# FFN of six batches as two-by-two blocks with seven products instead of eight, in float32, in a funnel attention and routed FFN kernel

## The chip, the cores and the metric

The kernel runs on one core of a Trainium2 chip. The metric is the device time of a launch in microseconds. TensorE multiplies matrices, VectorE, ScalarE and GpSimd work on elements, SyncE issues most DMAs. The profile's names for them are PE (with PEld for its weight loads), DVE, ACT, POOL and SP.

## The reference

Attention over pooled queries for 8 batches of 8 heads, then a feed-forward network (FFN) for the 128 tokens of each batch that a gate scores highest.

```python
# q, k, v: (8, 8, 1152, 64); w_gate (512), w1 (512, 1024), w2 (1024, 512); capacity 128; all float32
q_pool = q.reshape(B, H, S // 2, 2, D).mean(axis=3)
attn = softmax(scale * q_pool @ k.T)                 # 576 queries, 1152 keys
x = (attn @ v)  as (B, 576, 512)
scores = x @ w_gate
for b in range(B):
    top_idx = the 128 tokens with the highest scores[b]
    h = np.maximum(x[b, top_idx] @ w1, 0.0)          # 128 x 512 by 512 x 1024
    ye = h @ w2                                      # 128 x 1024 by 1024 x 512
    g = 1.0 / (1.0 + np.exp(-scores[b, top_idx]))
    out[b, top_idx] = x[b, top_idx] + g[:, None] * ye
```

## The kernel before

The main loop runs over 64 halves: two for each of the 32 pairs of heads (8 batches of 4 pairs). In half h, TensorE computes the scores of half h and then the weighted sums of half h-1. ScalarE takes exponentials from PSUM into `p` and copies the weighted sums out (`two`). GpSimd adds up exponentials (`acc`) for the softmax sums and adds the two parts of the weighted sums (`av`). VectorE folds the sums and transposes. Each batch's routing and FFN is a generator; `units()` advances every such generator by one step per half, up to its next true mark. Batch 5's second layer is held back for the end, where the last two batches' routing would otherwise leave TensorE idle. The function `pieces` then interleaves the three remaining generators: `older` (batch 5), `old` (batch 6) and `new` (batch 7). Each engine executes its instructions in the order in which this code emits them. Parts that the change and the prediction touch:

```python
        self.const = pool("const", 1)
        self.load = pool("load", 2)
        self.work = pool("work", 2)
        self.small = pool("small", 4)
        self.ffn = pool("ffn", 2)
        self.dram = pool("dram", 2, space=bass.MemoryType.DRAM)
        psum = bass.MemoryType.PSUM
        self.psum = pool("psum", 4, space=psum)
    # ... cut ...
    def load_pair(self, b, hp):

        nc = self.nc
        kb = self.load.tile([P, self.KB, BLK], F32, name="kb")
        qb = self.load.tile([P, self.QB, 2, BLK], F32, name="qb")
    # ... cut ...
        nc = self.nc
        qp = self.load.tile([P, self.QB, BLK], F32, name="qp", bufs=1)
        kT = pair["kT"] = self.load.tile([P, self.S], F32, name="kT")
        qT = pair["qT"] = self.load.tile([P, self.Sp], F32, name="qT")
        nc.gpsimd.tensor_tensor(
            out=qp[:, :, :], in0=pair["q"][:, :, 0, :], in1=pair["q"][:, :, 1, :], op=ALU.add
        )
        nc.vector.transpose(
            kT.rearrange("p (c g i) -> p c g i", c=self.NC, i=BLK),
            pair["k"].rearrange("p (g c) d -> p c g d", c=self.NC),
        )
        nc.vector.transpose(qT[:, :], qp.rearrange("p n d -> p (n d)"))
    # ... cut ...
        for c in range(self.NC):
            sc = self.banks()
            for e in range(2):
                keys = slice(e * self.D, (e + 1) * self.D)
                for j in range(2):
                    rows = slice(j * self.D, (j + 1) * self.D)
                    nc.tensor.matmul(
                        sc[keys, j, 0:n],
                        lhsT=pair["kT"][rows, c * P + keys.start : c * P + keys.stop],
                        rhs=pair["qT"][rows, qs],
                        start=True,
                        stop=True,
                    )
            nc.scalar.activation(p[:, c // G, c % G, :, :], sc[:, :, 0:n], AF.Exp, scale=self.scale)
    # ... cut ...
        two = self.small.tile([P, 2, n], F32, name="two", bufs=2)
        nc.scalar.copy(two[:, :, :], av[:, :, 0:n])
        half["av"] = self.small.tile([P, n], F32, name="av", bufs=2)
        nc.gpsimd.tensor_tensor(
            out=half["av"][:, :], in0=two[:, 0, :], in1=two[:, 1, :], op=ALU.add
        )
    # ... cut ...
            hT = ffn.tile([P, self.NFC, P], F32, name="hT")
            for f0 in range(0, self.NFC, 4):
                pv = self.banks()[:, 0, :].rearrange("p (c n) -> p c n", n=P)
                for f in range(4):
                    for c in range(self.ND):
                        nc.tensor.matmul(
                            pv[:, f, 0:w],
                            lhsT=self.w1[:, c, (f0 + f) * P : (f0 + f + 1) * P],
                            rhs=xeT[:, c, 0:w],
                            start=(c == 0),
                            stop=(c == self.ND - 1),
                        )
                    if f == 3:
                        nc.scalar.activation(hT[:, f0 : f0 + 4, 0:w], pv[:, :, 0:w], AF.Relu)
                    yield "hidden" if f0 + f == self.NFC - 1 else False
    # ... cut ...
            ps = self.banks()[:, 0, :]
            for f in range(self.NFC):
                nc.tensor.matmul(
                    ps[0:w, 0 : self.Dm],
                    lhsT=hT[:, f, 0:w],
                    rhs=self.w2[:, f, :],
                    start=(f == 0),
                    stop=(f == self.NFC - 1),
                )
                yield False
    # ... cut ...
                y = ffn.tile([P, self.Dm], F32, name="y", bufs=1)
                nc.scalar.activation(
                    y[0:w, :], ps[0:w, 0 : self.Dm], AF.Copy, scale=own_gate[0:w, 0:1]
                )
                nc.gpsimd.tensor_tensor(out=xe[0:w, :], in0=y[0:w, :], in1=xe[0:w, :], op=ALU.add)
            nc.gpsimd.indirect_dma_start(
    # ... cut ...
    def units(self):

        for entry in self.routing[::-1]:
            b, unit = entry
            if b in self.waiting:
                continue
            end = next((mark for mark in unit if mark), None)
            if end is None:
                self.routing.remove(entry)
            elif end == "hidden" and b == self.B - 3:
                self.waiting.add(b)
    # ... cut ...
                    if pair["hp"] == 0:
                        part = self.ffn.tile([P, self.NPAIR, self.QB], F32, name="part")
                    pair["part"] = part
                else:
                    loaded = None
                    if n + 2 < len(pairs):
                        loaded = self.load_pair(*pairs[n + 2])
                        self.load_values(loaded)
                    if n > 1:
                        self.stored(halves[h - 4]["pair"])
                if h > 1:
                    next(weights, None)
                half = {"pair": pair, "s": s}
                halves.append(half)
                self.scores(half)
                if h > 1:

                    of = halves[h - 2 - s]["pair"]
                    if s == 0:
                        of["groups"] = self.side_by_side(of["sum"].rearrange("p j n -> p (j n)"))
                    else:
                        self.spread(of)
                if h > 2:
                    self.gated(halves[h - 3])
                self.folded(half)
                if h > 1:
                    self.multiplied(halves[h - 2])
                if s == 0 and loaded:
                    upcoming = loaded
                    self.prepare_pair(upcoming)
            else:
                self.stored(halves[h - 3]["pair"])
                self.gated(halves[h - 3])
                self.multiplied(halves[h - 2])
                self.units()
            if h > 0:
                done = halves[h - 1]
                self.weighted(done)
                self.drained(done)
            if h == n_halves:
                self.multiplied(done)
                self.gated(halves[h - 2])
            if 1 < h < n_halves and s == 0:
                done["pair"]["total"] = self.added(done["pair"]["groups"])
            if h == n_halves:
                self.normalized(done["pair"])
            elif h > 2 and s == 1:
                self.normalized(halves[h - 2]["pair"])
            if h < n_halves:
                self.units()
    # ... cut ...
        pieces(older, self.NFC - 2)
        pieces(new, 1)
        pieces(older, 2)
        pieces(new, 3)
        pieces(older)
        pieces(old, self.NFC)
        pieces(new, 1)
        low = self.counted()
        pieces(old, self.NFC - 3)
        pieces(new, 2)
        pieces(old)
        count = self.outside(low)
        pieces(new)
```

## Time and profile before

| what | value |
|---|---|
| time, median of 3 runs (range) | 711.05 us (709.72 to 711.47) |
| span of the profiled execution, granted TensorE clock | 706.3 us, 0.999 |
| TensorE busy from 20 to 60, 200 to 600 us | all of it |
| TensorE busy from 690 to the end | 9.72 of 16.30 us |
| DMA | 82.86 MB, 376,640 of 389,490 packets under 512 B |
| exponentials (L825) | 576 of 128x576, 319.2 us |
| FFN layer 1 (L1203), layer 2 (L1216) on TensorE | 59.3 and 57.3 us |

A group line of the profile has the line of the kernel, the engine, the operation, output and inputs by name, shapes, the number of records, then busy microseconds, the mean nanoseconds of one, and the idle time of the engine before them with what ended it. A timeline line has the start, the time it takes, and the same names; "x72" means that 72 records in a row were merged. TensorE's ends are modelled, so its durations overlap.

### The profile page before, as it was taken

What the parts mean: (1) busy time and instruction counts of PE and PEld (TensorE: products, weight loads), DVE (VectorE), ACT (ScalarE), POOL (GpSimd) and SP (SyncE); (2) the same over time, 40 slices, a digit from 0 to 9 for tenths busy, and PEclk for the clock granted to TensorE, in tenths of its full rate; (3) what the DMA queues carried; (4) which work ended last, traced back from release to release, by engine and by line L of the source; (5) the groups of instructions that cost most, each with busy time, mean ns of one, the idle gap of its engine ahead of it and who ended that gap; (6) DMA issues with size and microseconds to landing.
All of it is one profiled execution on the core that took longest, in us unless ns stands there. A gap on an engine that the chain in (4) does not pass through costs nothing.

```text
span 706.3 us, 23391 instructions
## 1 busy us (share of the span) xinstructions
PE 695.8 (99%) x9948; PEld 499.9 (71%) x9948; DVE 494.4 (70%) x793; ACT 442.8 (63%) x963; POOL 484.9 (69%) x452
## 2 busy tenths in 40 slices
PE   8999999999999999999999999999999999999996
PEld 5668889977857678577775777767776677767573
DVE  3877777896549965499654987549784597869540
ACT  6677777777547774477745777467754777577210
POOL 5877777877668685586955879557884777866520
PEclk9999999999999999999999999999999999999999
DMA  9888887849692296825867258652877428442200
GB/s 181 172 170 181 182 166 139 151 95 164 116 169 57 66 165 126 154 52 106 166 104 135 52 126 159 119 106 52 163 127 134 86 53 172 72 82 60 47 31 35
DMA packets 389490, 82.86 MB, mean 117 GB/s; under 512 B 376640, under 2 KB 376640, under 8 KB 389376
## 3 DMA queue, kind: packets, MB, share of 16 engines
q1 hardware_dynamic: 387872, 76.49, 57.4%
q0 software_dynamic: 1280, 4.20, 1.7%
q8 instruction: 80, 1.31, 0.8%
q10 hardware_dynamic: 224, 0.59, 0.3%
q14 instruction: 34, 0.28, 0.1%
HBM read 69.65 MB, written 11.59 MB: 115 GB/s over the span
## 4 chain that ended last, share of the span: by engine, by line
PE 92%; POOL 3%; issue 1%; DVE 1%; DMA 1%; ACT 1%; SPq 0%; POOLq 0%; DVEq 0%; ACTq 0%
PE ps L818 38%; PE ps L836 37%; PE ps L1203 8%; PE ps L1216 7%; POOL acc L857 2%; DMA kb<-in_k_dram 1%; PE ps L1192 1%; POOL prod L925 0%; ACT p L825 0%; POOL x L956 0%; DVE fold L862 0%; POOL av L846 0%; SPq L759 0%; PE ps L1147 0%; PE ps L1053 0%
## 5 line engine op out<-in xcount | busy, mean ns | idle before, releaser
L825 ACT ACTIVATE p<-ps 128x576 f32<-128x576 f32 x576 | 319.2, 691 | 2.6 <-PE ps L818 2.3
L857 POOL TENSOR_TENSOR acc<-p 128x576 f32<-128x576 f32 x192 | 266.1, 1413 | 50.4 <-ACT p L825 50.0
L818 PE MATMUL ps<-qT,kT 64*64 64x288 f32 x4608 | 296.0, 405 | 0.3 <-ACT p L825 0.3
L836 PE MATMUL ps<-p,v_sb 64*64 64x288 f32 x4608 | 294.1, 403 | 0.0
L836 PEld LDWEIGHTS ps<-p,v_sb 64*64 64x64 f32 x4608 | 213.2, 133 | 67.8 <-ACT p L825 14.3
L818 PEld LDWEIGHTS ps<-qT,kT 64*64 64x64 f32 x4608 | 193.3, 132 | 89.8 <-ACT p L825 18.5
L862 DVE TRANSPOSE_TENSOR_REDUCE fold<-p 128x54 f32<-128x1728 f32 x64 | 126.0, 1969 | 117.2 <-ACT p L825 117.2
L862 DVE TRANSPOSE_TENSOR_REDUCE fold<-acc 128x54 f32<-128x1728 f32 x64 | 124.8, 1951 | 42.0 <-POOL acc L857 41.9
L844 ACT COPY two<-ps 128x576 f32<-128x576 f32 x64 | 40.9, 638 | 126.1 <-PE ps L836 113.2
L846 POOL TENSOR_TENSOR av<-two 128x288 f32<-128x288 f32 x64 | 51.1, 798 | 28.9 <-ACT two L844 27.3
L956 POOL TENSOR_TENSOR x<-avb,rec 128x576 f32<-128x576 f32 x32 | 37.0, 1157 | 43.1 <-DVE rec L954 27.1
L1203 PEld LDWEIGHTS ps<-xeT,w 128*128 128x128 f32 x512 | 57.8, 192 | 2.7 <-issue 2.6
L1203 PE MATMUL ps<-xeT,w 128*128 128x128 f32 x512 | 59.3, 277 | 0.0
L1216 PE MATMUL ps<-w,hT 128*128 128x512 f32 x128 | 57.3, 598 | 0.0
L925 POOL TENSOR_TENSOR prod<-avb,w_gate 128x288 f32<-128x288 f32 x64 | 51.3, 802 | 0.6 <-DVE avb L915 0.6
L902 ACT ACTIVATE sums<-total,tiny 32x18 f32<-32x18 f32 x124 | 38.2, 308 | 13.1 <-DVE total L893 11.4
L732 POOL TENSOR_TENSOR qp<-qb 128x576 f32<-128x576 f32 x31 | 43.8, 1412 | 2.5 <-DMA qb<-in_q_dram 2.5
L1216 PEld LDWEIGHTS ps<-w,hT 128*128 128x128 f32 x128 | 23.6, 190 | 28.1 <-issue 28.0
L735 DVE STREAM_TRANSPOSE kT<-kb 128x1152 f32<-128x1152 f32 x31 | 42.5, 1369 | 0.0
L1211 ACT ACTIVATE hT<-ps 128x512 f32<-128x512 f32 x16 | 9.6, 597 | 47.7 <-PE ps L1203 47.7
L1238 POOL TENSOR_TENSOR xe<-y,xe 128x512 f32<-128x512 f32 x7 | 8.9, 1270 | 38.3 <-ACT y L1235 38.3
L915 DVE STREAM_TRANSPOSE avb<-av 128x288 f32<-128x288 f32 x64 | 29.2, 456 | 7.2 <-POOL av L846 7.2
(95 smaller groups left out, 326.1 us busy)
## 6 DMA issues: line engine op xcount, KB each, us to landing
kb<-in_k_dram SPq DMA_DIRECT2D x124, 144.0 KB, 3.6
qb<-in_q_dram SPq DMA_DIRECT2D x124, 144.0 KB, 3.9
v_sb<-in_v_dram SPq DMA_DIRECT2D x124, 144.0 KB, 3.4
out_dram<-x SPq DMA_DIRECT2D x128, 72.0 KB, 3.0
lines<-row_rank SPq DMA_DIRECT2D x7, 640.0 KB, 4.1
w<-in_moe_w_dram SPq DMA_DIRECT2D x8, 512.0 KB, 4.8
sc_row<-row SPq DMA_DIRECT2D x7, 288.0 KB, 3.4
acc<-in_q_dram ACTq DMA_DIRECT2D x2, 288.0 KB, 4.2
```

The lines of the kernel that those rows point to most:

```text
L732: nc.gpsimd.tensor_tensor(out=qp[:, :, :], in0=pair["q"][:, :, 0, :], in1=pair["q"][:, :, 1, :], op=ALU.add)
L735: nc.vector.transpose(kT.rearrange("p (c g i) -> p c g i", c=self.NC, i=BLK), pair["k"].rearrange("p (g c) d -> p c g d", c=self.NC),)
L818: nc.tensor.matmul(sc[keys, j, 0:n], lhsT=pair["kT"][rows, c * P + keys.start : c * P + keys.stop], rhs=pair["qT"][rows, qs], start=True, ...
L825: nc.scalar.activation(p[:, c // G, c % G, :, :], sc[:, :, 0:n], AF.Exp, scale=self.scale)
L836: nc.tensor.matmul(av[j * self.D : (j + 1) * self.D, e, 0:n], lhsT=half["pair"]["v"][keys, j, c, :], rhs=half["p"][keys, c // G, c % G, j, :],
L844: nc.scalar.copy(two[:, :, :], av[:, :, 0:n])
L846: nc.gpsimd.tensor_tensor(out=half["av"][:, :], in0=two[:, 0, :], in1=two[:, 1, :], op=ALU.add)
L857: nc.gpsimd.tensor_tensor(out=acc[:, u, :], in0=units[:, 0, u, :], in1=units[:, 1, u, :], op=ALU.add)
L862: nc.vector.tensor_reduce(fold[:, a, :], of.rearrange("p u (m d) -> p (u m) d", d=BLK), AX.X, ALU.add, apply_transpose=True,)
L925: self.nc.gpsimd.tensor_tensor(out=pair["prod"][:, ns, :], in0=pair["avb"][:, ns, :], in1=self.w_gate[:, hp : hp + 1, :].broadcast_to([P, ...
L1203: nc.tensor.matmul(pv[:, f, 0:w], lhsT=self.w1[:, c, (f0 + f) * P : (f0 + f + 1) * P], rhs=xeT[:, c, 0:w], start=(c == 0), stop=(c == self ...
L1216: nc.tensor.matmul(ps[0:w, 0 : self.Dm], lhsT=hT[:, f, 0:w], rhs=self.w2[:, f, :], start=(f == 0), stop=(f == self.NFC - 1),)
```

## The change

Six of the eight batches' FFN is done for two batches at a time. The tokens of two batches are stacked into a matrix of 256 rows, and each of the two layers is a product of two matrices that are cut into two-by-two blocks. Such a product has eight block products; it can be written with seven, for sums and differences of blocks (Winograd's form of Strassen's scheme), all in float32. The sums of the weights (`tw`) are computed once by VectorE, kept in DRAM, and loaded for each layer; the sums of the inputs (`s`) are computed by GpSimd for each layer; ScalarE copies each product out of PSUM, and VectorE adds them in SBUF. Relu and the gate's scaling are separate ScalarE instructions on SBUF. To make room in SBUF, several tiles lose a buffer: `kb` and `qb` go from two to one, `v_sb` from three to two, `two`, `prod` and `sc_row` from two to one; V is loaded for the next pair instead of the one after it. Batches 4 and 5 now hold back their second layer together for the end, and the order of the pieces there is new. Batches 6 and 7 are computed as before. The purpose is to take multiplications off TensorE.

```diff
+
+        self.paired = self.B - 2 - self.B % 2
+        self.tw = self.const.tile([P, 4, self.ND // 2 * self.F // 2], F32, name="tw")
+        self.tw_kept = {}
 ... cut ...
 
+    def quarter(self, layer, i, j):
+
+        w, rows, columns = (self.w1, self.ND, self.F) if layer == 1 else (self.w2, self.NFC, self.Dm)
+        of = slice(i * rows // 2, (i + 1) * rows // 2), slice(j * columns // 2, (j + 1) * columns // 2)
+        return w[:, of[0], of[1]]
+
+    def summed(self, layer, i):
+        c = (self.ND if layer == 1 else self.NFC) // 2
+        return self.tw[:, i, :].rearrange("p (c n) -> p c n", c=c)
+
+    def weight_sums(self):
+
+        nc = self.nc
+        for layer in (2, 1):
+            b11, b12, b21, b22 = (self.quarter(layer, i, j) for i in range(2) for j in range(2))
+            t1, t2, t3, t4 = (self.summed(layer, i) for i in range(4))
+            kept = self.tw_kept[layer] = self.dram.tile(
+                [P, 4, self.tw.shape[-1]], F32, name=f"tw{layer}", bufs=1
+            )
+            for i, (to, x, y) in enumerate(((t1, b12, b11), (t2, b22, t1), (t3, b22, b12), (t4, b21, t2))):
+                nc.vector.tensor_tensor(out=to, in0=x, in1=y, op=ALU.subtract)
+                nc.sync.dma_start(kept[:, i, :], self.tw[:, i, :])
+                yield
+
+    def load_sums(self, layer):
+        for i in range(0, 4, 2):
+            self.nc.sync.dma_start(self.tw[:, i : i + 2, :], self.tw_kept[layer][:, i : i + 2, :])
+            yield
+
 
 
     def load_pair(self, b, hp):
 
         nc = self.nc
-        kb = self.load.tile([P, self.KB, BLK], F32, name="kb")
-        qb = self.load.tile([P, self.QB, 2, BLK], F32, name="qb")
+        kb = self.load.tile([P, self.KB, BLK], F32, name="kb", bufs=1)
+        qb = self.load.tile([P, self.QB, 2, BLK], F32, name="qb", bufs=1)
 ... cut ...
-        v_sb = pair["v"] = self.load.tile([P, 2, self.NC, self.D], F32, name="v_sb", bufs=3)
+        v_sb = pair["v"] = self.load.tile([P, 2, self.NC, self.D], F32, name="v_sb", bufs=2)
 ... cut ...
-        two = self.small.tile([P, 2, n], F32, name="two", bufs=2)
+        two = self.small.tile([P, 2, n], F32, name="two", bufs=1)
 ... cut ...
+            token = {"xe": xe, "xeT": xeT, "gate": own_gate, "index": index, "rows": rows_out, "w": w, "b": b}
+            if b >= self.paired:
+                yield from self.layers(token)
+            elif b % 2 == 0:
+                self.first_of_two = token
             else:
-                y = ffn.tile([P, self.Dm], F32, name="y", bufs=1)
-                nc.scalar.activation(
-                    y[0:w, :], ps[0:w, 0 : self.Dm], AF.Copy, scale=own_gate[0:w, 0:1]
-                )
-                nc.gpsimd.tensor_tensor(out=xe[0:w, :], in0=y[0:w, :], in1=xe[0:w, :], op=ALU.add)
-            nc.gpsimd.indirect_dma_start(
-                out=rows_out,
-                out_offset=bass.IndirectOffsetOnAxis(ap=index[0:w, 0:1], axis=0),
-                in_=xe[0:w, :],
-                in_offset=None,
-                bounds_check=(b + 1) * Sp - 1,
-                oob_is_err=False,
-            )
+                yield from self.layers_of_two([self.first_of_two, token])
 ... cut ...
+    def room_of_sums(self, c, w):
+        s = self.ffn.tile([P, 4, self.NFC // 2, P], F32, name="s", bufs=1)
+        return s, [s[:, i, 0:c, 0:w] for i in range(4)]
+
+    def input_sums(self, a, s):
+
+        a11, a12, a21, a22 = a
+        s1, s2, s3, s4 = s
+        add, subtract = ALU.add, ALU.subtract
+        for i, (to, x, y, op) in enumerate(
+            ((s1, a21, a22, add), (s2, s1, a11, subtract), (s3, a11, a21, subtract), (s4, a12, s2, subtract))
+        ):
+            self.nc.gpsimd.tensor_tensor(out=to, in0=x, in1=y, op=op)
+            if i % 2:
+                yield i == 3
+
+    def seven_products(self, layer, a, s, c, rest, shape):
+
+
+
+        nc = self.nc
+        (a11, a12, _, a22), (s1, s2, s3, s4), (c11, c12, c21, c22) = a, s, c
+        b11, b21, b22 = (self.quarter(layer, i, j) for i, j in ((0, 0), (1, 0), (1, 1)))
+        t1, t2, t3, t4 = (self.summed(layer, i) for i in range(4))
+        u, x, y = rest
+
+        steps = (
+            (a11, b11, c11, ()),
+            (s2, t2, u, ((u, c11),)),
+            (s3, t3, c21, ((c21, u),)),
+            (s1, t1, c22, ((u, c22), (c22, c21))),
+            (s4, b22, c12, ((c12, u),)),
+            (a12, b21, x, ((c11, x),)),
+            (a22, t4, y, ((c21, y),)),
+        )
+        for i, (of, by, to, sums) in enumerate(steps):
+            if i % 2 == 0:
+                tile = self.banks()
+            ps, n = shape(tile[:, i % 2, :]), of.shape[1]
+            for f in range(by.shape[2] // P if layer == 1 else 1):
+                for k in range(n):
+                    if layer == 1:
+                        args = ps[:, f, :], by[:, k, f * P : (f + 1) * P], of[:, k, :]
+                    else:
+                        args = ps, of[:, k, :], by[:, k, :]
+                    nc.tensor.matmul(
+                        args[0], lhsT=args[1], rhs=args[2], start=k == 0, stop=k == n - 1
+                    )
+            nc.scalar.copy(to, ps)
+            for to, of in sums:
+                nc.vector.tensor_tensor(out=to, in0=to, in1=of, op=ALU.add)
+            yield i == len(steps) - 1
+
+    def layers_of_two(self, tokens):
 ... cut ...
+        a = quarters([token["xeT"] for token in tokens], self.ND // 2)
+        _, s = self.room_of_sums(self.ND // 2, w)
+        for _ in self.input_sums(a, s):
             yield True
+        hidden = [ffn.tile([P, self.NFC, P], F32, name="hT") for _ in tokens]
+        c = quarters(hidden, self.NFC // 2)
+        rest = [ffn.tile([P, 512], F32, name="u", bufs=1)]
+        rest += [ffn.tile([P, 512], F32, name="y") for _ in range(2)]
+        yield from self.seven_products(1, a, s, c, [lines(tile) for tile in rest], lines)
+        for tile in hidden:
+            nc.scalar.activation(tile[:, :, 0:w], tile[:, :, 0:w], AF.Relu)
+        loads = self.load_sums(2)
+        next(loads)
+        yield True
+        for _ in loads:
+            pass
+        room, s = self.room_of_sums(self.NFC // 2, w)
+        for last in self.input_sums(c, s):
+            yield "hidden" if last else True
+        half = self.Dm // 2
+        ys = [ffn.tile([P, self.Dm], F32, name="y") for _ in tokens]
+        rest = ffn.tile([P, self.Dm], F32, name="u", bufs=1)
+
+        def halves(tile):
+            return [tile[0:w, i * half : (i + 1) * half] for i in range(2)]
+
+
+        over = room[:, 1].rearrange("p c n -> p (c n)")
+        yield from self.seven_products(
+            2,
+            c,
+            s,
+            halves(ys[0]) + halves(ys[1]),
+            halves(rest) + halves(over)[0:1],
+            lambda bank: bank[0:w, 0:half],
+        )
+        for token, y in zip(tokens, ys):
+            nc.scalar.activation(y[0:w, :], y[0:w, :], AF.Copy, scale=token["gate"][0:w, 0:1])
+        yield True
+        for token, y in zip(tokens, ys):
+            xe = token["xe"]
+            nc.gpsimd.tensor_tensor(out=xe[0:w, :], in0=y[0:w, :], in1=xe[0:w, :], op=ALU.add)
+            self.written(token)
+            yield True
+        if tokens[1]["b"] + 1 < self.paired:
+            for _ in self.load_sums(1):
+                yield True
 ... cut ...
-            self.load_values(loaded)
         self.load_gate()
         weights = self.weight_loads()
+        sums = self.weight_sums() if self.paired else iter(())
         for h in range(n_halves + 1):
             if h < n_halves:
                 n, s = divmod(h, 2)
@@ -1322,11 +1477,14 @@
                     loaded = None
                     if n + 2 < len(pairs):
                         loaded = self.load_pair(*pairs[n + 2])
-                        self.load_values(loaded)
+                    if n + 1 < len(pairs):
+                        self.load_values(upcoming)
                     if n > 1:
                         self.stored(halves[h - 4]["pair"])
                 if h > 1:
                     next(weights, None)
+                if h > 10 and s == 1:
+                    next(sums, None)
 ... cut ...
-        pieces(older, self.NFC - 2)
+        pieces(older, 3)
         pieces(new, 1)
-        pieces(older, 2)
+        pieces(older, 1)
         pieces(new, 3)
+        pieces(older, 3)
+        pieces(old, self.NFC // 2 - 1)
         pieces(older)
-        pieces(old, self.NFC)
         pieces(new, 1)
         low = self.counted()
-        pieces(old, self.NFC - 3)
+        pieces(old, self.NFC // 2 + 1)
         pieces(new, 2)
         pieces(old)
         count = self.outside(low)

```

## The prediction

> **What bounds the kernel now.** I read the page's busy shares first, then the chain of work that ended last, then the groups by line, then the timeline of a few stretches.
>
> ```profile
> PE 695.8 (99%) x9948; PEld 499.9 (71%) x9948; DVE 494.4 (70%) x793; ACT 442.8 (63%) x963; POOL 484.9 (69%) x452
> ...
> PE 92%; POOL 3%; issue 1%; DVE 1%; DMA 1%; ACT 1%; SPq 0%; POOLq 0%; DVEq 0%; ACTq 0%
> ...
> L1203 PE MATMUL ps<-xeT,w 128*128 128x128 f32 x512 | 59.3, 277 | 0.0
> L1216 PE MATMUL ps<-w,hT 128*128 128x512 f32 x128 | 57.3, 598 | 0.0
> ```
>
> TensorE is busy for 99% of the span and 92% of the last chain runs through it, so removing its work pays one for one, as long as no wait takes its place. The FFN is 116.6 of its 695.8 us. The mean durations (277 and 598 ns) overlap; real spacing comes from the timeline: one batch's layer 1, 64 records, takes 7.41 us, 0.116 each; layer 2 has a weight load every 0.43 us, 16 records, 6.9 us with its end. Each float32 matmul has two records (256 and 64 matmuls gave 512 and 128).
>
> How closely ScalarE is tied to TensorE decides this case. A plain half of a head pair, in the timeline:
>
> ```profile
> 231.36 4.59 PE L818 MATMUL ps<-qT,kT 64*64 64x288 f32 x72
> 231.68 0.64 ACT L844 COPY two<-ps 128x576 f32<-128x576 f32 x1 [1.91 <-PE ps L836]
> ...
> 232.32 4.98 ACT L825 ACTIVATE p<-ps 128x576 f32<-128x576 f32 x9
> ...
> 235.72 4.60 PE L836 MATMUL ps<-p,v_sb 64*64 64x288 f32 x72
> ```
>
> Scores start, 0.96 us later the nine exponentials start, and 4.36 us after the scores the weighted sums start. Now a half where ScalarE has something more to do between `two` and the exponentials:
>
> ```profile
> 257.92 0.64 ACT L844 COPY two<-ps 128x576 f32<-128x576 f32 x1 [1.27 <-PE ps L836]
> 258.34 5.00 PE L818 MATMUL ps<-qT,kT 64*64 64x288 f32 x72
> 258.58 0.85 ACT L887 COPY groups<-line 32x18 f32<-32x18 f32 x4
> 259.34 0.57 ACT L1195 COPY xeT<-ps 128x512 f32<-128x512 f32 x1
> 259.82 4.90 ACT L825 ACTIVATE p<-ps 128x576 f32<-128x576 f32 x9
> ...
> 263.17 4.69 PE L836 MATMUL ps<-p,v_sb 64*64 64x288 f32 x72
> ```
>
> The exponentials start 1.48 us after the scores, 0.52 later than above, and the weighted sums start after 4.83 us, 0.47 later. With four PSUM tiles for scores TensorE runs only four chunks ahead. The slack is about 0.05 us: extra ScalarE work at this place stops TensorE nearly one for one, although the 99% doesn't show it.
>
> The tail, from the same view:
>
> ```profile
> 659.38 1.16 POOL L956 TENSOR_TENSOR x<-avb,rec 128x576 f32<-128x576 f32 x1 [1.51 <-DVE rec L954]
> ...
> 661.24 0.79 POOL L846 TENSOR_TENSOR av<-two 128x288 f32<-128x288 f32 x1
> ...
> 665.81 1.21 PE L1053 MATMUL ps<-diag,ones 128*128 128x288 f32 x4 [0.38 <-DVE rank_parts L1075]
> ...
> 678.35 1.05 POOL L1178 DMA_INDIRECT xe<-out_dram,index  x1 [5.14 <-ACT own_gate L1155]
> ```
>
> After the last attention (about 660) other batches' FFN fills TensorE while GpSimd, VectorE and ScalarE route batch 7. TensorE waits 0.38 us for its scores at 665.8, and the gather of its tokens starts at 678.35, 1.95 us after the ranks' `pick` ends (676.40). This fit is tight.
>
> [...] `part` (L981, 128x18) takes 178 ns at least but 892 in the median. [...]
>
> **The change part by part.**
>
> 1. TensorE loses work. Layer 1 of two batches: 7 products of 8 matmuls are 112 records, 12.97 us against 14.82: 1.85 saved. Layer 2: [...] 1.5 saved. Three pairs of batches: 3 x 3.35 = 10.0 us saved.
>
> 2. ScalarE gains copies. The seven copies of a layer lie beside the products (0.6 us each for 512 columns, `hT`'s duration, against 1.85 us a product), and the last is over 0.75 us after the last product, before the exponentials' usual start. They cost TensorE nothing. But the two relus over 128x1024 come one half later, after `two` and ahead of the exponentials: the exact place shown above. An exponential over 576 columns takes 0.553 us in a row (4.98/9); at that rate 1024 columns take 0.98, two relus 1.97, less 0.05 of slack: 1.9 us lost, three times: 5.7. The two scalings of `y` (128x512, some 0.5 each) stand at the same place in the two earlier pairs: 2 x 1.0 = 2.0. Before, relu and scaling directly followed long FFN stretches, where ScalarE was idle.
>
> 3. VectorE gains seven additions a layer (about 0.6 us for 512 columns, half for 256, from 0.76 for `diag` of 576), some 14 us in all plus GpSimd's hold-ups, and eight weight differences of 1024 columns, about 1.1 us each. The first lie in FFN stretches where VectorE has caught up; at 70% busy I count them as hidden.
>
> 4. GpSimd gains four input sums a layer: for 512 columns 1.27 us each (`xe`'s duration), for 256 about 0.72: 24 us in all. In the loop they take up its slack (some 1.7 us a half outside the FFN). `two` has one buffer now, so a late `av` would stop ScalarE. I allow 1.5 us in all.
>
> 5. Buffers and loads. `kb` and `qb` have one buffer, so a pair's K is issued only after the previous `kT` transpose, 10 to 16 us into a pair's first half, and V comes last in the queue. Issue takes 4.3 us each for K and Q and 2.5 for V; landing 3.5. From 11.4 us on, V lands at about 26.5 where the sums need it at 30.6. It fits, but less so where routing delays VectorE, and in the first 100 us where weights share DMA engines 82 to 89% busy. I allow 1.5 us. Sums kept in DRAM (4 MB written, 10 MB read) are few large pieces against a 57% share.
>
> 6. The tail. Layer 2 of batches 4 and 5 now lies wholly there; that moves work from the loop and costs nothing by itself. But the order of instructions shows two new waits. First, the four 512-wide sums stand on GpSimd ahead of the last `av`, so the chain to batch 7's scores starts 4 x 1.27 = 5.1 us later, while TensorE has three products (5.3 us) to fill it, about as much as now (5.4). Some 4.0 us idle. Second, ScalarE's scaling of `y` stands before `index` and `own_gate`, and GpSimd has two `xe` additions and two writes (2 x 1.27 + 2 x 1.04, with gaps about 5) ahead of batch 7's gather. The gather starts some 7 us after the pick, not 1.95, and lands 3.6 later; TensorE has left 20 matmuls of layer 1 (4.6 us) by then and puts the transposes ahead of the remaining layer 2. Some 4.2 us idle. With 0.4 for small waits and less the present 1.0, the tail costs 7.6.
>
> Sum: 711.05 - 10.0 + 5.7 + 2.0 + 1.5 + 1.5 + 7.6 = 719.35. Two of the smaller allowances may be zero, so I put it at **718 us**.
>
> **Rivals.** (a) TensorE stays the bound everywhere: if ScalarE had slack at the relus and the tail filled itself, only the 10.0 count: 701. The 99% speaks for it; the xeT half and the instruction order speak against. (b) Single buffers starve it: if K, Q or V come late in every pair, a microsecond or two in 30 pairs makes 740 or more. The issue queue's own waits of 70.6 us for the weighted sums (V's buffer) show that loads already run against buffers; that TensorE nowhere waits for V speaks against. (c) VectorE or GpSimd becomes the bound: 494 + 14 + 9 and 485 + 24 stay under 75%, so only runs of crowded halves could do this; 722 to 730. (d) Only the tail goes wrong and the loop keeps its savings: 709.
>
> **Range and chances.** The saving is sure within 1 us, the relu and scaling term within 2, the tail within 3, the loads are open upwards. I take 708 to 729. Faster by 2% would need 696.8, below even rival (a): 0.01. Slower by 2% is over 725.3, which takes a part of (b) or (c): 0.13. The rest is 0.86.
>
> **What would show it.** FFN busy spacing: records of 256 columns about 0.22 us apart. Relu halves: exponentials about 2.9 us after the scores and weighted sums some 6.3 us after them. The tail: a gap on TensorE of about 4 us before the 128x288 score matmuls, named after VectorE, and another before the last token transposes, with GpSimd's two writes ahead of the gather. K, Q and V: hardly any TensorE idle named after a DMA. I am wrong if the relu halves show no delay (then ScalarE has room I don't see), if batch 7's gather isn't behind the writes, or if idle time spreads over all pairs.

## The result, and the profile after

The changed kernel takes 757.57 us (median of 4 runs, 757.04 to 762.22) against 710.7 before: a ratio of 1.0671 [1.0633, 1.071]. It is 6.7% slower, where 708 to 729 was predicted. The profiled execution is the slowest of the four (762.22 us). Its page, with busy times, the granted clock in 40 slices, and the shares of the chain that ended last:

```profile
PE 707.5 (93%) x9972; PEld 526.3 (69%) x9972; DVE 529.6 (70%) x842; ACT 462.4 (61%) x999; POOL 511.6 (67%) x475
...
PEclk9999999999999899999999999999999989999989
...
PE 57%; POOL 15%; issue 7%; DVE 7%; DMA 5%; ACT 4%; SPq 3%; POOLq 0%; DVEq 0%; ACTq 0%
```

TensorE went from 99% busy to 93%, and its share of the last chain from 92% to 57%. GpSimd, which had 3% of the chain before, has 15%. Three slices have a lower clock. The span grew from 706.3 to 760.5 us; idle time of TensorE grew from 10.5 to 53.0. What it waited for, from the view of waits (total us, times, longest):

```profile
PE ps L1221 <- DMA xe<-out_dram,index: 8.0, 2, 6.0
PE ps L847 <- ACT p L854: 6.9, 6, 1.4
PE ps L1339 <- ACT hT L1342: 5.6, 8, 0.8
PE ps L847 <- ACT two L873: 4.8, 4, 2.0
PE ps L1049 <- DVE line L1035: 4.8, 1, 4.8
PE ps L847 <- ACT xeT L1224: 4.1, 4, 1.3
PE ps L1082 <- DVE lines L1072: 2.3, 1, 2.3
PE ps L1339 <- ACT y L1342: 2.3, 5, 0.5
```

Four families stand here: block products waiting for copies (L1339; 10.1 us with further rows of 1.5 and 0.7 that are not shown), scores waiting for exponentials behind relus and scalings (6.7 of the 6.9 on `p`), the routing of single batches (`two`, `xeT`, `line`, one `xe` of 2.0, with 1.3 for V's loads and 0.5 for `qT` that are not shown; 17.5), and the tail (6.0 and 2.3, with 0.7 for the picks: 9.0). Only the second and the fourth had been predicted with their causes.

The first family, in the timeline of TensorE in the first pair's layer 1:

```profile
285.97 2.05 PE L1339 MATMUL ps<-xeT,w 128*128 128x128 f32 x16
288.79 3.81 PE L1339 MATMUL ps<-s,tw 128*128 128x128 f32 x32 [0.77 <-ACT hT L1342]
293.27 2.05 PE L1339 MATMUL ps<-s,tw 128*128 128x128 f32 x16 [0.68 <-ACT hT L1342]
...
297.79 2.05 PE L1339 MATMUL ps<-xeT,w 128*128 128x128 f32 x16 [0.68 <-ACT hT L1342]
```

Products 2, 4 and 6 wait; 3, 5 and 7 do not. Products 1 and 2, 3 and 4, and 5 and 6 share a PSUM tile (`if i % 2 == 0: tile = self.banks()`), and each second one waits until ScalarE has copied the first. ScalarE's copy takes 0.59 us (`hT<-ps` 288.06 to 288.65), and only then product 2 starts.

The second family is as predicted, TensorE first, then ScalarE:

```profile
310.34 2.12 PE L847 MATMUL ps<-qT,kT 64*64 64x288 f32 x32
313.90 2.88 PE L847 MATMUL ps<-qT,kT 64*64 64x288 f32 x40 [1.44 <-ACT p L854]
```

```profile
311.30 2.00 ACT L1367 ACTIVATE hT<-hT 128x1024 f32<-128x1024 f32 x2
313.21 4.96 ACT L854 ACTIVATE p<-ps 128x576 f32<-128x576 f32 x9
```

The two relus (2.00 us) stand ahead of the exponentials, which start 2.87 us after the scores (predicted: about 2.9), and TensorE stops for 1.44 us.

The tail, TensorE:

```profile
702.80 1.21 PE L1082 MATMUL ps<-lines,ones 128*128 128x288 f32 x4 [2.35 <-DVE lines L1072]
...
729.23 1.09 PE L1221 MATMUL ps<-ident,xe 128*128 128x128 f32 x4 [6.01 <-DMA xe<-out_dram,index]
730.11 9.46 PE L1256 MATMUL ps<-w,hT 128*128 128x512 f32 x16
```

Both waits that the prediction named are there. GpSimd ahead of the second one:

```profile
719.65 1.28 POOL L1398 TENSOR_TENSOR xe<-y,xe 128x512 f32<-128x512 f32 x1
722.16 1.00 POOL L1285 DMA_INDIRECT out_dram<-xe,index  x1 [1.23 <-DMA out_dram<-xe,index]
725.71 1.06 POOL L1207 DMA_INDIRECT xe<-out_dram,index  x1 [2.54 <-DMA out_dram<-xe,index]
```

The gather (third line) stands behind the additions and writes, as predicted. But the second write also waits 1.23 us for the first to land, and the gather 2.54 us for the second.

The third line of TensorE's timeline above is something else: the 8 products (16 records) of batch 6's layer 2 take 9.46 us, where those of batch 7, right after, take 7.03. The trace records the granted clock. From 7.9, 257.1, 441.4, 622.3, 717.9 and 728.1 us on it stands at one half for 3.41 or 6.83 us, 30.7 us in all up to its last product, each time in idle time or shortly behind it. Not every idle time does this: 1.99, 0.68 and 1.28 us at 175 to 180 and 2.35 at 703 left the clock full, and the stretch at 717.9 follows a wait of only 0.68 us and ten records of two columns. Before had none until 705.1 us, behind its last product.

### The profile page after: what moved, and what is told of

It is laid out like the page before. It is cut to its first block, busy times and chain, and to the rows that moved or that the text cites. A ratio compares the mean times of both kernels' runs of the same rounds, so it can differ in the third digit from the quotient of the medians.

```text
span 760.5 us, 23543 instructions
## 1 busy us (share of the span) xinstructions
PE 707.5 (93%) x9972; PEld 526.3 (69%) x9972; DVE 529.6 (70%) x842; ACT 462.4 (61%) x999; POOL 511.6 (67%) x475
## 4 chain that ended last, share of the span: by engine, by line
PE 57%; POOL 15%; issue 7%; DVE 7%; DMA 5%; ACT 4%; SPq 3%; POOLq 0%; DVEq 0%; ACTq 0%
PE ps L847 22%; PE ps L865 22%; POOL acc L886 9%; PE ps L1339 9%; DVE fold L891 4%; DMA kb<-in_k_dram 2%; PE ps L1256 2%; ACT p L854 2%; SPq L736 1%; DVE kT L764 1%; POOL av L875 1%; POOL prod L954 1%; PE ps L1243 1%; POOL x L985 1%; SPq L739 1%
## 5 line engine op out<-in xcount | busy, mean ns | idle before, releaser
L847 PE MATMUL ps<-qT,kT 64*64 64x288 f32 x4608 | 309.1, 414 | 16.4 <-ACT p L854 6.9
L886 POOL TENSOR_TENSOR acc<-p 128x576 f32<-128x576 f32 x192 | 269.8, 1434 | 77.8 <-ACT p L854 77.5
L865 PE MATMUL ps<-p,v_sb 64*64 64x288 f32 x4608 | 296.9, 403 | 1.4 <-DMA v_sb<-in_v_dram 1.3
L847 PEld LDWEIGHTS ps<-qT,kT 64*64 64x64 f32 x4608 | 202.6, 135 | 107.4 <-ACT p L854 33.2
L865 PEld LDWEIGHTS ps<-p,v_sb 64*64 64x64 f32 x4608 | 219.4, 133 | 65.8 <-ACT p L854 13.7
L916 ACT COPY groups<-sum 32x36 f32<-32x36 f32 x124 | 27.0, 218 | 26.4 <-DVE sum L901 24.9
L1008 DVE TENSOR_REDUCE red<-prod 128x9 f32<-128x288 f32 x64 | 27.6, 432 | 0.4 <-POOL prod L954 0.4
L1199 POOL TENSOR_SCALAR index<-found_token 128x1 int32<-128x1 f32 x7 | 6.4, 919 | 28.5 <-DVE pick L1190 28.5
L1010 DVE TENSOR_TENSOR part<-red,rec 128x18 f32<-128x18 f32 x32 | 23.3, 728 | 1.1
L1342 ACT COPY y<-ps 128x256 f32<-128x256 f32 (+1 forms) x18 | 8.0, 444 | 26.0 <-PE ps L1339 26.0
L901 DVE TENSOR_REDUCE sum<-fold 128x18 f32<-128x108 f32 x64 | 21.9, 341 | 2.2
```

The lines of the kernel that those rows point to most:

```text
L847: nc.tensor.matmul(sc[keys, j, 0:n], lhsT=pair["kT"][rows, c * P + keys.start : c * P + keys.stop], rhs=pair["qT"][rows, qs], start=True, ...
L865: nc.tensor.matmul(av[j * self.D : (j + 1) * self.D, e, 0:n], lhsT=half["pair"]["v"][keys, j, c, :], rhs=half["p"][keys, c // G, c % G, j, :],
L886: nc.gpsimd.tensor_tensor(out=acc[:, u, :], in0=units[:, 0, u, :], in1=units[:, 1, u, :], op=ALU.add)
```

## The experiments

Each differs from the changed kernel ("after") unless told otherwise. Ratios are to the kernel before, run beside it. Executions of one kernel differ by up to 10 us (748.26 and 758.83 in experiment 10), and many experiments have only two; so for effects of a few microseconds the waits in the trace say more than the medians.

**1. Buffers alone.** After's buffers and order of loads, with the old FFN for every batch and the old end.

```diff
-        self.paired = self.B - 2 - self.B % 2
+        self.paired = 0
 ... cut: the old order of the pieces ...
```

> The changed kernel's buffers and load order with the old FFN: no batch is paired, so no weight sums, no input sums, no seven products, and the old order of the last pieces. If single K and Q buffers with the later loads make the routing late (theory): TensorE idles before the token transposes and in the half after them for 1.3 to 5 us per batch as in the changed kernel (175, 242 to 258, 439, 624 us), 16 us idle and some 8 us of halved clock there: 725 to 735. If VectorE's extra work makes the routing late (rival): within 3 us of the kernel before, 708 to 714.

713.18 us, 1.0052 [1.004, 1.0064]. Fewer buffers and later loads cost 3.6 us with the old FFN. That they make the routing late was my first theory for the third family, and it fell: of the waits at routing only 2.00 us at 607 are here. The prediction's rival (b) falls with it as far as it blamed single buffers.

**2. A PSUM tile for each product.**

```diff
-            if i % 2 == 0:
-                tile = self.banks()
-            ps, n = shape(tile[:, i % 2, :]), of.shape[1]
+            tile = self.banks()
+            ps, n = shape(tile[:, 0, :]), of.shape[1]
```

> The changed kernel, but each of the seven products has a PSUM tile of its own instead of two sharing one. Theory: the second product of a tile waits for ScalarE's copy of the first, 3 x 0.71 us a layer 1 and 3 x 0.48 a layer 2, 10.7 us in all; these waits vanish, 745 to 749. Rival (seven products are slow on TensorE itself, by their weight loads): the gaps stay and the time is within 2 us of 757.

745.52 us, 1.0506 [1.047, 1.0541]: 12.0 us less. The same stretch of TensorE's timeline in this run:

```profile
280.94 2.05 PE L1338 MATMUL ps<-xeT,w 128*128 128x128 f32 x16
282.83 5.52 PE L1338 MATMUL ps<-s,tw 128*128 128x128 f32 x48
```

Products 2 to 4 follow one another without a bracket, and so it goes on: every wait of the first family is gone. It was the shared tile: the copies and ScalarE's work are the same in this run.

**3. No weight differences on VectorE** (left out; zeros stand in their place and are stored and reloaded as before).

> The changed kernel without VectorE's eight weight differences (the sums of the weights are zeros, so the seven products compute something else; all transfers stay). Theory: they lengthen only the routing of the first two batches, so 3 to 6 us less, 751 to 755, and the stalls at about 439 and 624 us stay. Rival (VectorE's extra work is what makes the routing late): 15 us or more less, 742 or below.

754.78 us, 1.0636 [1.0549, 1.0724]. The waits at routing stay (1.79 + 1.28 us at 176, 1.90 + 1.28 at 253, 1.21 + 1.28 at 435, 4.36 at 619), so VectorE's differences are not their cause. The time is within the expectation, but 752.36 and 757.20 are too far apart to give the 2.8 us a size.

**4. Relus on VectorE**, at the same place (`nc.vector.tensor_scalar(... op0=ALU.max)`).

> The changed kernel with the relus of the paired batches on VectorE at the same place of the program instead of ScalarE. Theory: three stalls of 1.44 us after the relu vanish, 752 to 754. Rival (ScalarE has room there, the stall has another cause): the stalls stay, within 1.5 us of 757.

755.85 us, 1.0651 [1.0601, 1.0702]. All three waits of 1.44 us are gone, so the mechanism holds, but only 1.7 of 4.3 us came back, less than expected: layer 2's second product now waits 1.55 us `<-POOL index L1199` twice in the loop (0.51 in after), and the waits of the tail grow to 3.70 and 7.62.

**5 to 7. Bunching.** After postpones the even batch's FFN, so odd batches are routed in halves without FFN. Experiment 5 does that with the old eight products and after's buffers, 6 with before's buffers, 7 spreads after's FFN instead.

```diff
-                yield from self.layers_of_two([self.first_of_two, token])
+                for mark in self.layers(self.first_of_two):
+                    yield True if mark == "hidden" else mark
+                yield from self.layers(token)
 ... cut: no sums of weights; in 6 the old buffers ...
```

```diff
+        if tokens[1]["b"] + 1 < self.paired:
+            for _ in range(4):
+                yield True
         loads = self.load_sums(2)
```

> The eight products of before, no copies, no additions, no weight differences, with the buffers of after; only the feed-forward network of batches 0, 2 and 4 is put off and done directly ahead of that of batch 1, 3 and 5, as after does it. Theory (putting it off makes each odd batch's routing fall into halves without feed-forward products, where VectorE, GpSimd and the row queue do not keep up, and TensorE idles and its clock is halved): the idle times at the routing of batches 1, 3 and 5 and stretches of half clock appear as in after, 8 to 20 us above the 713.2 of the kernel with the same buffers and no delay, 721 to 733. Rival (the delay is harmless; the stalls come of the added work of GpSimd, VectorE and ScalarE): 711 to 717, with no half clock in the loop.

720.51 us, 1.0169 [1.0109, 1.023].

> The same delay with the buffers and the load order of before (two k and q buffers, values loaded a pair earlier, two buffers of the gathered copies). Theory that delay and single buffers act together: 709 to 715, the stalls of the run with single buffers shrink to a third. Theory that the delay alone does it: within 4 us of the run with single buffers.

719.13 us, 1.015 [1.0119, 1.018].

> After, with four halves more between layer 1 and layer 2 of the first two pairs of batches, so that feed-forward work comes every eight halves or so, as before had it. Theory (halves without feed-forward work are those in which the other engines fall behind): the idle times at 433 to 441 and at 617 to 624 us shrink to under 1.5 us together, and the half clock at 442 and 623 us goes; 744 to 751. Rival (how the work is spread does not matter): within 3 us of 757.6.

756.22 us, 1.0673 [1.0642, 1.0704]. In 5 and 6 the loop hardly waits (0.99 us at 418 and 1.49 at 590 in 5, nothing in 6); about 6 us of waits stand in the tail, whose order is after's, with 6.8 and 10.2 us at half clock. In 7, 3.61 + 1.28 us at 434 and 6.41 at 619 are there as ever. The bunching theory fell.

**8. Another order at the end.** The last pair's sums for layer 2 one step earlier; batch 7's gather ahead of the scaling and writing of batches 4 and 5, into a `p` tile that is free by then.

```diff
 ... cut: the gather's tile, the earlier sums ...
-        pieces(older)
         pieces(new, 1)
+        pieces(older)
```

> After, with the order at the end changed: the last pair's sums for layer 2 are put out one step earlier, the gather of batch 7 goes to GpSimd ahead of the scaling and writing of batches 4 and 5, into a buffer that is free. Theory (the waits of 2.35 and 6.01 us at the end are queueing of VectorE and GpSimd behind the last pair and set the end, and the half clock after them costs some 3 to 5 us more): both waits under 1.5 us, 746 to 752. Rival (the gather lands no earlier because the ranking that feeds it is late anyway): the wait on the gather stays above 4 us, 754 to 758.

743.43 us, 1.0493 [1.0403, 1.0582]: 14.1 us less. The wait of 2.35 is 0.52, that of 6.01 is gone:

```profile
716.48 7.03 PE L1260 MATMUL ps<-w,hT 128*128 128x512 f32 x16
```

The layer-2 products are back at 7.03 us. 7.8 us of waits (less 1.5 for a new one on `sum`) and 10.2 us at half clock went there. The run makes both changes at once.

**9. TensorE kept busy in the tail's wait**, with six products into PSUM that nobody reads.

```diff
+            if b == self.B - 1:
+                spare = self.banks()
+                for _ in range(6):
+                    nc.tensor.matmul(
+                        spare[:, 0, :], lhsT=self.ident, rhs=self.w1[:, 0, 0:512], start=True, stop=True
+                    )
```

> After, with six products of 128 x 512 whose results nobody reads put on TensorE directly ahead of the last transposes, so that it is busy in the 6.01 us in which it waited for the gather. Nothing else changes; the gather lands when it did. Theory (the half clock after the wait is caused by TensorE's being idle): the stretch of half clock at 728.7 us goes, the 16 layer-1 products of the last batch take about 7.0 us instead of 9.25, 753.5 to 756. Rival (the clock falls for another reason, or the busy work costs as much): 757 to 760.

```profile
722.28 0.63 PE L1227 MATMUL ps<-ident,xe 128*128 128x128 f32 x4 [0.91 <-DMA xe<-out_dram,index]
722.75 7.03 PE L1262 MATMUL ps<-w,hT 128*128 128x512 f32 x16
```

The gather is as late as in after (a wait of 0.91 us behind 5.32 us of the added products) and the work the same, yet the 16 records of layer 2 (the expectation calls them layer 1) take 7.03 us instead of 9.46 and the transposes 0.63 instead of 1.09: idleness caused the half clock. In the eight other runs that keep this wait (2 to 4, 7, 10 to 13; 6.08 to 7.71 us), 6.8 us at half clock follow it each time. The times do not decide (757.08 lies with the rival, but they run from 752.44 to 760.67): 2.9 us drown in what the other waits vary by.

**10. No stores of weight differences during routing** (differences left out; zeros in their place are stored in halves 3 and 5).

> No differences of weights and none of their eight stores in the loop: the sums of weights are zeros, stored as two zero blocks in the third and fifth half, before any routing. Theory (the 524 KB store that goes to the queue directly ahead of the row of ranks makes that row late, and with it index, accumulation, fold and exponentials): the idle times of 1.99 + 0.68 + 1.28 us at 175 to 180 us and of about 5 us at 242 to 258 us go, those at 440 and 624 stay; 746 to 751. Rival (the stores are harmless, as leaving out VectorE's differences alone was): 753 to 757, all the idle times stay.

753.54 us, 1.0636 [1.0546, 1.0725]. The waits at 175 to 180 and at 242 to 258 are gone, those at 434 (2.69 + 1.28) and 620 (4.40) stay, as the theory had it. Experiment 3 left out the differences alone and kept these waits, so it is the stores. The total does not reach the expected 746 to 751 and is blurred: V is late at 93 us (2.84), behind four issues of K that take 12.68 us after a 2 MB store. This is after's queue at batch 0:

```profile
156.50 0.57 SPq L719 DMA_DIRECT2D tw<-tw  x1
157.17 0.39 SPq L1155 DMA_DIRECT2D row_rank<-both  x1
160.56 0.32 SPq L1159 DMA_DIRECT2D lines<-row_rank  x1
```

A 512 KB store goes out directly ahead of the row of ranks; the row's reload is issued 3.39 us after the row, 2.13 in experiment 1, and its users run late.

**11 and 12. y scaled and added by one VectorE instruction** for each token (`scalar_tensor_tensor`, y times gate plus `xe`), first beside each write, then for both tokens a half earlier. What it is meant to relieve, GpSimd in after:

```profile
377.15 1.27 POOL L1398 TENSOR_TENSOR xe<-y,xe 128x512 f32<-128x512 f32 x1
378.70 1.05 POOL L1285 DMA_INDIRECT out_dram<-xe,index  x1 [0.28 <-DMA out_dram<-x]
```

> After, with the scaling of y on ScalarE and its addition on GpSimd replaced by one VectorE instruction for each token (y times gate plus xe). Theory (the two additions of 1.27 us and the writes keep GpSimd full from 376 to 396 us, so it is 2 to 3 us late when the ranking of the odd batch begins, and that stays until its exponentials): the 1.29 + 1.29 us at 440 and half of the 4.77 us at 624 go, with most of the half clock there, and the two waits of 1.18 us for exponentials too; 746 to 751. Rival (VectorE is as full as GpSimd there, so work moved to it delays as much): only the 2 x 1.18 go, 754 to 756.

751.13 us, 1.0602 [1.0535, 1.0668]. Only the two waits of 1.18 us and 1.8 of the 4.77 (now at 618) went, and those at 436 grew to 2.33 + 1.19: the second write now stands 3.03 us in GpSimd's queue waiting for VectorE, with the accumulation behind it.

> As the run in which VectorE scales and adds y, but for both tokens one half ahead of the writes, so that no write in GpSimd's queue waits for VectorE. Theory (GpSimd's queue behind the y additions and the writes is what makes the odd batch's ranking late): now the idle times at 436 and 618 us shrink to under 1.5 and 2 us with GpSimd free some 2.5 us earlier; 745 to 749. Rival (it is the reload of the sums of weights, 4.2 MB on the queue from 396 us on, or the single buffers): they stay at 2.3 to 3 us, 750 to 755.

748.88 us, 1.055 [1.0506, 1.0594]. GpSimd is on time, but 2.00 + 1.14 us at 433 and 3.60 at 614 stay. That the waits stay is the rival's forecast, though the time lies in the theory's 745 to 749. SyncE's queue, then GpSimd, in this run:

```profile
393.84 1.10 SPq L724 DMA_DIRECT2D tw<-tw  x2
396.60 9.29 SPq L736 DMA_DIRECT2D kb<-in_k_dram  x4
...
415.28 0.57 SPq L1155 DMA_DIRECT2D row_rank<-both  x1
```

```profile
422.65 0.92 POOL L1199 TENSOR_SCALAR index<-found_token 128x1 int32<-128x1 f32 x1 [7.32 <-DVE pick L1190]
```

The ranks are ready at 408.4. But behind the reload of the sums of weights (2 MB) the next four issues of K take 9.29 us (5.49 and 6.24 in after's two such places, 3.72 in experiment 5, which reloads nothing), so the row goes out at 415.3 and VectorE's pick waits 4.43 us for it. GpSimd, in order, holds the accumulation (at 425.02) behind the index: fold, total, reciprocal, `two` and exponentials follow late. By this reading two causes feed the same chain, and taking one away lets the other through. No run leaves out the reload alone, so its part is read from the queue and not shown by an experiment.

**13. Picks, index and gather a half later**, one half less between gather and transposes (batches 0 to 5).

```diff
                 yield True
+                if b < self.B - 2:
+                    yield True
 
                 found = self.small.tile([P, 1], F32, name="found_token")
 ... cut: one half less after the gather ...
```

> After, but for batches 0 to 5 VectorE's picks, GpSimd's index and the gather come one half later, and one of the two halves between the gather and its transposes is left out, so that the transposes stay where they were. Theory (GpSimd works in order; the index that waits for the row of ranks stands ahead of the accumulation, and so the late row holds up accumulation, fold, total, reciprocal, exponentials and TensorE; with a half more time the row is always there): all idle times on two and xeT at 174 to 180, 242 to 258 and 440 go or fall under 0.5 us, the 4.77 at 624 falls too, and the half clock there; 16 to 20 us less, 738 to 742. Rival (the other engines are simply too full in these halves, whatever the order): within 4 us of 757.6, the waits only move.

754.96 us, 1.0641 [1.0622, 1.066]. `two` and `xeT` are gone as waits (0.2 us is left of each), so GpSimd's order was the link. But the half taken away was needed: TensorE waits 3.56, 3.18, 3.94 and 2.33 us for the gathers themselves. The expected 738 to 742 fell for that.

**14 to 16. All repairs together.** 14: own tiles, relus by quarter as each is whole, experiments 8 and 11, the differences in the other half of each pair. 15: own tiles, relus by quarter, 8, 12 and 13, with the last pair's sums on VectorE. 16: as 15, but batches 0 to 4 keep both halves after the gather, the last pair's sums follow its relus directly, and more of batch 6's layer 1 stands ahead of the last picks.

> All repairs at once: a PSUM tile for each product, relus of a quarter as soon as it is whole instead of at the next half, y scaled and added by one VectorE instruction, the end's order changed, the differences and their stores put into the other half of each pair of heads. If the costs found are separate and add up: 757.6 - 12 (own tiles) - 14 (end) - 4.3 (relus) - 2.4 (y) - 3 to 12 (routing, with its half clock) = 713 to 722. If what is left of routing keeps its size when the rest is faster: 722 to 728. To beat before it would have to come under 707.

731.66 us, 1.0322 [1.0288, 1.0356].

> Own PSUM tile for each product, relus by quarter, y scaled and added early on VectorE, the end's order changed with the last pair's sums for layer 2 on VectorE, and the picks and gather a half later. The run with all repairs but the last two took 731.7; its idle times at routing add up to 14.0 us with 3.4 us more for half clock, and 4 to 6 us at the end. If they go: 708 to 715. If only those of two go: 716 to 722. Under 706 it would beat before.

719.47 us, 1.0157 [1.0118, 1.0195].

> As the last combination, which took 719.5 and still had 3.45 and 3.31 us for gathers at 176 and 251, 1.45 and 1.37 at 424 and 594, 3.31 on VectorE's sum at 660 (one addition of the last pair's sums took 6.57 us on VectorE beside GpSimd's accumulation) and 1.40 on the picks at 680, with 6.8 us more at half clock there. Now batches 0 to 4 keep both halves between gather and transposes, the last pair's sums stand directly behind its relus, where GpSimd has nothing to do, and 16 more layer-1 products of batch 6 stand ahead of the last picks. If the accounting is right: 719.5 - 8.2 - 3.3 - 1.4 - 5 to 7 for half clock = 700 to 704, which is faster than before (709.6). If the half clock or other waits take their place: 706 to 714.

714.45 us (711.97 to 716.99 in 6 runs), 1.0088 [1.0066, 1.011]: of the 6.7% that the change cost, 5.8 points are back, but it does not beat before. Run 14 lies above both of its expectations, so the gains of single repairs did not simply add up; 15 lies in its second, and 16 just above its second. Lines of run 16's page and, from the groups by line and shape, the scores:

```profile
PE 689.5 (97%) x9972; PEld 507.4 (71%) x9972; DVE 548.2 (77%) x852; ACT 458.0 (64%) x999; POOL 503.1 (71%) x465
...
PEclk9999999999999999999999999999999999999999
...
L847 PE MATMUL ps<-qT,kT 64*64 64x288 f32 x4608 | 300.9, 407 | 6.7 <-ACT p L854 3.0 <-ACT two L873 2.9 <-DVE qT L768 0.9
```

The clock is full. Idle time is 21.0 us, 10.5 more than before, nearly all of it in waits of 0.4 to 2.2 us. Scores and weighted sums count as busy for 300.9 + 295.2 us, 6.0 more than before's 296.0 + 294.1 for the same products; waits too short to be listed are a possible reading, not shown. Those 16.5 us eat the saving.

## Why the prediction was wrong

In order of the prediction's parts, with what the runs put in their place:

| part | predicted | found |
|---|---|---|
| 1, TensorE's work | -10.0 | -11.5 |
| 2, copies | 0 ("They cost TensorE nothing") | 10.1 of waits; 12.0 by experiment 2 |
| 2, relus and `y` | 5.7 + 2.0 | 4.3 + 2.4 |
| 3 to 5, VectorE, GpSimd, loads | 0 + 1.5 + 1.5 | 17.5 of waits |
| 6, tail | 7.6 | 8.0 of waits (9.0 less before's 1.0) |
| clock | no term | up to 15.4 (estimate, half of 30.7: the 4.9 us at half clock in the 9.46 us cost 2.43) |

The found waits and the saving make 30.8; the clock takes it to at most 46.2 of the 54.2 us between the two profiles. The idle time is accounted for: it grew by 42.5 us, and the found waits make 42.3. What is missing lies inside TensorE's busy records, which grew by 11.7 us although the FFN lost 11.5. Of those 23.2 us the clock explains at most 15.4, and less where half clock falls into a wait or ahead of one: the stretch at 718 ends before the gather's 6.01 us and can only have shortened them. Scores and weighted sums hold 15.9 us of the growth (309.1 + 296.9 against 296.0 + 294.1). Why run 16, with a full clock, still has 6.0 us of it stays open.

**Part 1 was right.** One batch before, then a pair of batches in run 16, where the waits are gone, each time up to the scores that follow:

```profile
267.79 7.41 PE L1203 MATMUL ps<-xeT,w 128*128 128x128 f32 x64
275.13 4.59 PE L818 MATMUL ps<-qT,kT 64*64 64x288 f32 x72
...
284.02 7.13 PE L1216 MATMUL ps<-w,hT 128*128 128x512 f32 x16
291.09 4.59 PE L818 MATMUL ps<-qT,kT 64*64 64x288 f32 x72
```

```profile
285.51 2.05 PE L1345 MATMUL ps<-xeT,w 128*128 128x128 f32 x16
...
298.21 2.17 PE L847 MATMUL ps<-qT,kT 64*64 64x288 f32 x32
...
334.79 1.99 PE L1345 MATMUL ps<-w,hT 128*128 128x256 f32 x8
...
347.07 3.14 PE L847 MATMUL ps<-qT,kT 64*64 64x288 f32 x48
```

A batch takes 7.34 us for layer 1 and 7.07 for layer 2, two batches 28.82; a pair takes 12.70 and 12.28, together 24.98. Three pairs save 3 x 3.84 = 11.5. The predicted 1.5 us for layer 2 was the author's estimate, as before has no records of 256 columns: run 16's came 0.219 us apart (12.28 / 56), and the line between before's 0.116 for 128 columns and 0.429 for 512 (L1216's weight loads from 284.56 to 290.14 us) gives an estimate of 0.220. The work was saved; it never reached the end.

**Part 2 failed in its first step.** The prediction compared durations, 0.6 us of copying against 1.85 of product, and concluded that they lie beside each other. For three of the seven that fails: two products share a tile, as the diff shows, and the second waits until the first has been copied. So each even product starts after a whole copy, and the time is copy plus hand-over, 0.77 and 0.68 us in layer 1, 0.51 and 0.46 in layer 2. The sentence on relus and scalings was right in place and mechanism and a little high in size: 1.44 for 1.9, 1.18 for 1.0. Experiment 4 shows why a right term is not yet a gain to be had: its three waits went, and others grew.

**Parts 3 to 5 failed as sums of small allowances.** VectorE's term was also too small: seven additions a layer at the prediction's 0.6 and 0.3 us make 18.9 us and not "some 14", and they took 24.5 in after; its differences took 1.2 to 1.8 us each, not 1.1. But size was not the failure. Each engine by itself had room (VectorE 70%, GpSimd 67%), and each resource alone was cheap: buffers 3.6 us (1), differences no more than some 3 (3). The prediction added such costs. But routing is a chain over all of them: ranks on VectorE, a row through the queue, picks, an index in GpSimd's queue ahead of the accumulation. The change put a store ahead of the row (10), additions and writes ahead of the ranks (11), and a reload ahead of the next loads (12). The part of the store, at 175 to 180 and 242 to 258 us, is shown by experiments 3 and 10. How much each of the other two has in the waits at 440 and 624 us is open. Rival (b), 740 or more, was nearest by its time, but for another reason: not single buffers in every pair, but large transfers and the queue's order at single batches. "Few large pieces against a 57% share" was the wrong measure for a queue in which the next small row waits behind the piece (ready at 408.4 us, sent at 415.3 in experiment 12).

**Part 6 was right in place and cause, and partly lucky in its sum**: predicted 4.0 and 4.2 us of idle, measured 2.35 and 6.01, so that two errors of some 1.7 us cancel. Both causes (four sums on GpSimd ahead of the last `av`, two additions and writes ahead of the gather) fit experiment 8, which takes both away and both waits with them. What made the second wait longer is the landing of the writes, 1.23 and 2.54 us, which the prediction did not count: the gather starts 10.3 us after the pick, not 7.

**No part priced the clock.** In after it stands at one half for 3.41 or 6.83 us at a time, and the wait ahead of it can be short: behind 1.79 + 1.28 us within 4 us it was halved at 178 us in experiment 3 (5.81 us from the scores' restart to the weighted sums), while 1.99, 0.68 and 1.28 at the same place in after left it full (3.20 us). The prediction has no term for it, while it foresaw two gaps of 4 us; before's trace, with a full clock up to 705.1 us, did not show it.

## What to carry to other kernels

Fewer products need not make a kernel faster where the results then need copies: count what stands between a product's end and the next use of its PSUM tile, and give each product its own. Before adding traffic or element work to a kernel whose TensorE is 99% busy, follow the longest chain over other engines and queues, and ask what will stand ahead of its smallest items. And a gap of a few microseconds on TensorE can cost more than itself, as the products behind it may run at half clock (9.46 us instead of 7.03 behind the wait of 6.01).

## What the runs showed of the hardware

- The granted clock fell to one half for 3.41 or 6.83 us in or shortly behind some idle times (6.83 at the wait of 6.01 us in after, none at its 2.35), and products that nobody reads prevented it (7.03 instead of 9.46 us for the same 16 records).
- A VectorE addition of two SBUF inputs was held up ninefold beside GpSimd. In run 15, VectorE, then GpSimd:

```profile
648.09 0.69 DVE L1313 TENSOR_TENSOR s<-s,hT 128x512 f32<-128x512 f32 x1
648.70 6.57 DVE L1313 TENSOR_TENSOR s<-hT 128x512 f32<-128x512 f32 x1
```

```profile
649.09 4.12 POOL L886 TENSOR_TENSOR acc<-p 128x576 f32<-128x576 f32 x3
...
653.93 0.79 POOL L875 TENSOR_TENSOR av<-two 128x288 f32<-128x288 f32 x1
```

  The addition of the same size took 6.57 us instead of 0.69: it ended 0.55 us after GpSimd's last of five instructions in a row. In run 16, with GpSimd idle, all four of these additions took 0.68 to 0.69. That it waited for these five is how this one trace reads. Before's `part` (128x18), also of two SBUF inputs, took 0.18 us at 618.35 with GpSimd idle, and 0.92 at 600.43, until 0.03 us after the end of GpSimd's `x` (600.16 to 601.32).
- A float32 copy out of PSUM by ScalarE took 0.59 us for 512 columns and 0.37 for 256, so half the columns took 63% of the time; 2 x 1024 columns from SBUF took 2.00.
